# Loads that transpose, two channels in one matmul, and the plane sums moved into a 128-row contraction: one change of three parts to an attention and S4 kernel

## The chip, the cores and the metric

The kernel runs on one core of one Trainium2 chip. The metric is the device time of one execution in microseconds (us), median of several runs. Fast executions of a kernel agreed within about 1.5% here. The "granted clock" is the share of TensorE's full clock that the profile shows as allowed; in the traces here it is 1.00 or 0.5 at any moment, and a mean over a stretch lies between. "PE" is TensorE, "DVE" is VectorE, "ACT" is ScalarE, "POOL" is GpSimd and "SP" is SyncE, whose queue issues most of the loads.

## The reference, cut to what matters

The output joins two independent halves of 640 columns each.

```python
# half A: local dilated attention (32 heads of 20, window 8, dilation 2), S = 2048
qkv = x @ wqkv                                   # x [2048, 640]: needs x transposed for TensorE
o   = softmax(q . k_window * scale) . v_window;  a = o @ wo
# half B: S4 convolution, 640 channels d, 192 states n
K[d, l] = Re( sum_n C[d,n] * exp(dt*A)[d,n]**l * dt*B[d,n] )     # 2048 taps per channel
y = irfft( rfft(u, 4096) * rfft(K, 4096) )[:2048] + u * Dskip
```

The exponent `l` is rounded to bf16 before it is used, so many of the 2048 taps coincide. The kernel computes only distinct ones: a tap is a sum over n of X[n, a] * Y[n, b], with a table X of 20 powers and a table Y of 33 powers per channel, both complex and in bf16. So every channel costs TensorE a few very small matmuls: weights X (20 columns), moving data Y (33 columns). A matmul that needs only some of the 128 columns of TensorE's array can be placed on a part of them, a "column tile" of 32 or 64 columns (`tile_position` in the code). PSUM is the memory that matmuls write; ACT copies results out of it ("evictions").

## The kernel before

It works on five chunks of 128 channels (32 channels on each of four partition groups). Per chunk, DVE makes the tables X and Y; PE makes the taps (`kgen`); PE does a Fourier transform in two steps (`f1`, `f2_prod`); DVE multiplies the spectra of u and K; PE inverts (`ia`). The attention is interleaved with the chunks. A preparation stage of about 140 us comes first: parameters are loaded and flipped by PE ("flips", tile `ps_tr`), x is loaded and transposed by PE (`ps_xt`), projections of x are made (`ps_p`), and "generators" compute the tables' base powers. The order of instructions on each engine is not the order of the text: a scheduler decides it from modelled times, and then every engine executes in that order.

```python
def kgen(tc, pools, X, Y, Kd):                   # X [128, 20, 2, 192], Y [128, 33, 2, 192]
    for nt in (11, 11, 10):
        ps = psum.tile([128, nt, NB], f32, name="ps_k")
        MM(ps[:], lhsT=zw, rhs=Y[:, 0:nt, 0, 0:NB], start=True, stop=False)        # clears the bank
        for part in range(4):                    # real and imaginary; rows 0..127, then the last 64
            for i in range(nt):
                for g in range(4):
                    o = ps[32 * g:32 * g + 20, i, :]
                    if part < 2:
                        col = 32 * g + t0 + i
                        MM(o, lhsT=X[:, :, part, col], rhs=Y[:, :, part, col], ..., tile_position=(0, 32 * g))
                    else:
                        ...                      # 64 rows, tile_position=(hb, 32 * g)
        nc.scalar.copy(out=Kd[:, :, t0:t0 + nt], in_=ps[:]...)
    ...
# f2_prod: after S (both spectra, bf16) has been copied from PSUM by ACT
    V.tensor_tensor(out=Y, in0=K, in1=Ur..., op=A.mult)
    V.tensor_tensor(out=t[:], in0=K, in1=Ui..., op=A.mult)
    V.tensor_tensor(out=Y[:, :, 0], in0=Y[:, :, 0], in1=t[:, :, 1], op=A.subtract)
    V.tensor_tensor(out=Y[:, :, 1], in0=Y[:, :, 1], in1=t[:, :, 0], op=A.add)
# ia: weights of 32 columns, one column tile per group
            for r in range(2):
                for g in range(4):
                    MM(o, lhsT=Yf[:, :, r, 4 * j + g], rhs=C["EA"][:, r, :], ..., tile_position=(0, 32 * g))
# load and transpose
        for q in range(8):
            xn = xw.tile([128, 2, D], bf16, name="xn", bufs=3)
            nc.sync.dma_start(out=xn[:], in_=xsrc[:, 2 * q:2 * q + 2, :])
        ...                                      # later: 80 PE matmuls by the identity, 24 ACT copies into xT
```

The softmax here doesn't subtract the row's maximum and nothing guards it: scores larger than these inputs give would overflow.

Of the kernel before, what the change touches and what calls it, by code (L numbers as in the profile page):

```python
# [18 lines left out]
CW = 192  # L19
MAGIC = 12582912.0  # L20
# [8 lines left out]
X_EXP = [0, 4, 2, 6, 1, 5, 3, 7, 256, 260, 258, 262, 512, 516, 768, 772, 1024, 1280, 1536, 1792]  # L29
NB = 33  # L30
# [7 lines left out]
def sel_consts_np():  # L38
# [9 lines left out]
    def add(W):  # L48
        full = np.zeros((128, 128), np.float32)
        for g in range(4):  # L50
            full[32 * g:32 * g + 32, 32 * g:32 * g + 32] = W
        mats.append(full)
        return len(mats) - 1

    for j in range(8):
        Ws = {}
        for s in range(8):
            for be in range(32):
                p = 256 * s + 8 * be + j
                bhi, blo = be // 8, be % 8  # L60
                hit = [(i, b) for (i, b) in look[int(r[p])] if b == be or (b == be + 1 and i >= 8)]
                i, b = sorted(hit, key=lambda q: q[1])[0]
                W = Ws.setdefault((bhi, be % 2), np.zeros((8, 32, 32), np.float32))
                W[blo, i + 12 * (b - be), 4 * s + bhi] = 1.0
# [16 lines left out]
def fft_consts_np():  # L81
# [11 lines left out]
    EA = np.zeros((128, 2, 64, 2, 2))  # L93
    for dd in range(2):
        s = slice(64 * dd, 64 * dd + 64)
        EA[s, 0, :, 0, dd] = np.cos(phi)
        EA[s, 0, :, 1, dd] = np.sin(phi)
        EA[s, 1, :, 0, dd] = -np.sin(phi)
        EA[s, 1, :, 1, dd] = np.cos(phi)
    psi = 2 * np.pi * (l1[None, None, :] * k1[:, None, None] / 64 + l0[None, :, None] * k1[:, None, None] / 4096)  # L100
    HB = np.zeros((128, 64, 2, 128))
    for g in range(4):
        s = slice(32 * g, 32 * g + 32)
        HB[s, :, 0, s] = 2 * np.cos(psi) / 4096
        HB[s, :, 1, s] = -2 * np.sin(psi) / 4096
    return dict(BD1=BD1.reshape(128, 256), T=T.reshape(128, 32 * 2 * 64), EA=EA.reshape(128, 512), HB=HB.reshape(128, 64 * 2 * 128))


def partB_prep(tc, pools, prm, Gd):
# [29 lines left out]
    def flip(a, diag, tag="l"):  # L139
        psb = [psp.tile([128, 512], f32, name="ps_tr", tag=tag, bufs=2 if tag == "l" else 3) for _ in range(2)]  # L140
        for c in range(NCH):
            rhs = dg[:, c, :] if diag else ident[:]
            for h in range(2):
                hs = slice(64 * h, 64 * h + 64)
                col = c * CW + 64 * h
                nc.tensor.matmul(psb[col // 512][:, col % 512:col % 512 + 64], lhsT=nat[a][:, c, 0:128], rhs=rhs[:, hs], start=True, stop=True, skip_group_check=True)
            for h in range(2):
                hs = slice(64 * h, 64 * h + 64)
                col = c * CW + 128
                nc.tensor.matmul(psb[col // 512][hs, col % 512:col % 512 + 64], lhsT=nat[a][hs, c, 128:192], rhs=rhs[hs, hs], start=True, stop=True,  # L150
                                 tile_position=(64 * h, 64 * h), skip_group_check=True)
        return [(slice(0, 512), psb[0][:]), (slice(512, W), psb[1][:, 0:W - 512])]
# [62 lines left out]

def cmul(nc, O, Y, g, t, conj, rep=None):

    V = nc.vector
    sh = list(Y.shape)
    gr, gi = (g[:, r] for r in range(2))  # L220
    for _ in range(2):
        gr, gi = gr.unsqueeze(1), gi.unsqueeze(1)
    full = lambda ap: ap.rearrange("p a n r m -> p a (n r) m") if rep else ap
    gb = lambda ap: ap.to_broadcast([sh[0], sh[1], sh[2] * 2 if rep else 2, sh[-1]])
    V.tensor_tensor(out=full(O), in0=full(Y), in1=gb(gr), op=A.mult)  # L225
    V.tensor_tensor(out=full(t), in0=full(Y), in1=gb(gi), op=A.mult)  # L226
    P = [O[:, :, r] if not rep else O[:, :, :, r] for r in range(2)]
    T = [t[:, :, r] if not rep else t[:, :, :, r] for r in range(2)]
    V.tensor_tensor(out=P[0], in0=P[0], in1=T[1], op=(A.add if conj else A.subtract))  # L229
    V.tensor_tensor(out=P[1], in0=P[1], in1=T[0], op=(A.subtract if conj else A.add))  # L230


def table_tiles(pools):
    tp = pools["tab"]
    return (tp.tile([128, 20, 2, CW], bf16, name="Xtab", tag="Xtab", bufs=2), tp.tile([128, 6, 2, CW], bf16, name="Xg", tag="Xg"),
# [3 lines left out]
def tables(tc, pools, tiles):  # L239
# [3 lines left out]
    tmp = pools["tab"].tile([128, 8, 2, CW], bf16, name="krtmp", tag="krtmp")  # L243
# [3 lines left out]
    def xs(o, i, g):  # L247
        n = len(range(20)[i])
        cmul(nc, X[:, o], X[:, i], Xg[:, g], tmp[:, 0:n], True)

    S_ = slice
    xs(S_(1, 2), S_(0, 1), 2)
    xs(S_(2, 4), S_(0, 2), 1)
    xs(S_(4, 8), S_(0, 4), 0)
    xs(S_(8, 12), S_(0, 4), 3)
    cmul(nc, X[:, 12:16].rearrange("p (a b) r m -> p a b r m", a=2), X[:, 0:16].rearrange("p (a b) r m -> p a b r m", a=2)[:, :, 0:2], Xg[:, 4],
         tmp[:, 0:4].rearrange("p (a b) r m -> p a b r m", a=2), True, rep=2)
    xs(S_(16, 18), S_(0, 9, 8), 5)
    xs(S_(18, 20), S_(12, 15, 2), 5)
    for k in range(1, 5):  # L260
        n = 2 ** k - 1
        for i in range(0, n, 8):
            m = min(8, n - i)
            cmul(nc, Y[:, n + 2 + i:n + 2 + i + m], Y[:, 1 + i:1 + i + m], Y[:, n + 1], tmp[:, 0:m], False)
# [3 lines left out]
def kgen(tc, pools, X, Y, Kd):  # L268
    nc = tc.nc
    MM = nc.tensor.matmul  # L270
    t0 = 0
    for nt in (11, 11, 10):
        ps = pools["psum"].tile([128, nt, NB], f32, name="ps_k", tag="k", bufs=1)
        MM(ps[:], lhsT=pools["zw"], rhs=Y[:, 0:nt, 0, 0:NB], start=True, stop=False, skip_group_check=True)
        for part in range(4):
            for i in range(nt):
                for g in range(4):
                    o = ps[32 * g:32 * g + 20, i, :]
                    if part < 2:
                        col = 32 * g + t0 + i  # L280
                        MM(o, lhsT=X[:, :, part, col], rhs=Y[:, :, part, col], start=False, stop=False,  # L281
                           tile_position=(0, 32 * g), skip_group_check=True)
                    else:
                        col = 128 + 32 * (g % 2) + t0 + i
                        hb = 64 * (g // 2)
                        MM(o, lhsT=X[hb:hb + 64, :, part - 2, col], rhs=Y[hb:hb + 64, :, part - 2, col], start=False, stop=(part == 3),  # L286
                           tile_position=(hb, 32 * g), skip_group_check=True)
        nc.scalar.copy(out=Kd[:, :, t0:t0 + nt], in_=ps[:].rearrange("p t b -> p b t"))  # L288
        t0 += nt
    for g in range(4):  # L290
        r = 32 * g
        nc.gpsimd.dma_start(out=Kd[r + 20:r + 32, 0:NB - 1, :].rearrange("p b t -> p (b t)"), in_=Kd[r + 8:r + 20, 1:NB, :].rearrange("p b t -> p (b t)"))  # L292
# [35 lines left out]
def f2_prod(tc, pools, C, A1, Yf):  # L328
# [5 lines left out]
    for b in range(4):  # L334
        S = fp.tile([128, 8, 2, 2, 64], bf16, name="S", tag="S", bufs=2)
        for h in range(4):
# [7 lines left out]
            nc.scalar.copy(out=S[:, 2 * h:2 * h + 2], in_=ps[:])  # L344
        Y = Yf[:, 8 * b:8 * b + 8]
        K, Ur, Ui = S[:, :, :, 1, :], S[:, :, 0, 0, :], S[:, :, 1, 0, :]
        t = fp.tile([128, 8, 2, 64], bf16, name="pt", tag="pt", bufs=2)
        V.tensor_tensor(out=Y, in0=K, in1=Ur.unsqueeze(2).to_broadcast([128, 8, 2, 64]), op=A.mult)
        V.tensor_tensor(out=t[:], in0=K, in1=Ui.unsqueeze(2).to_broadcast([128, 8, 2, 64]), op=A.mult)
        V.tensor_tensor(out=Y[:, :, 0], in0=Y[:, :, 0], in1=t[:, :, 1], op=A.subtract)  # L350
        V.tensor_tensor(out=Y[:, :, 1], in0=Y[:, :, 1], in1=t[:, :, 0], op=A.add)


def ia(tc, pools, C, Yf, Z):
    nc = tc.nc
    MM = nc.tensor.matmul
    for jq in range(8):
        ps = pools["psum"].tile([128, 2, 64, 2, 2], f32, name="ps_ia", tag="b", bufs=3)
        for jj in range(2):
            j = 2 * jq + jj  # L360
            for r in range(2):
                for g in range(4):
                    o = ps[32 * g:32 * g + 32, jj].rearrange("p l r d -> p (l r d)")
                    MM(o, lhsT=Yf[:, :, r, 4 * j + g], rhs=C["EA"][:, r, :], start=(jj == 0 and r == 0), stop=(r == 1), skip_group_check=True, tile_position=(0, 32 * g))  # L364
# [13 lines left out]
class PartA:  # L378
# [8 lines left out]
    def load(self):  # L387
        nc, xw = self.nc, self.pools["xw"]
        xsrc = self.x[0].rearrange("(st p) k -> p st k", p=128)
        self.xn = []  # L390
        for q in range(8):
            xn = xw.tile([128, 2, D], bf16, name="xn", tag="xn", bufs=3)
            nc.sync.dma_start(out=xn[:], in_=xsrc[:, 2 * q:2 * q + 2, :])
            self.xn.append(xn)
# [7 lines left out]

    def transpose(self):
        nc, xw = self.nc, self.pools["xw"]
        self.xT = xT = xw.tile([128, 5, S], bf16, name="xT")
        for q in range(8):
            for kp in range(3):
                kn = 2 if kp < 2 else 1
                ps = self.psp.tile([128, 2, 2, 128], f32, name="ps_xt", tag="a", bufs=2)
                for kk in range(kn):  # L410
# [334 lines left out]
```

## Time and profile before

| | before |
|---|---|
| time | 511.86 us, median of 3 runs (510.85 over the 4 fast ones taken with the change) |
| PE / DVE / ACT busy, share of the span | 72% / 70% / 53% |
| granted TensorE clock, mean | 0.876 |
| first multiply of a table / first product of spectra | 58 us / 200 us |
| last tap matmul / end | 381.5 us / 511 us |

The busy line of the profile's page comes first, then the first steps of ACT and SP. In a timeline the columns are start, length, engine, line, operation, output <- input, shapes and count; the bracket tells how long the engine was idle and who released it.

```profile
...
PE 368.9 (72%) x5943; PEld 243.2 (48%) x5943; DVE 360.2 (70%) x528; ACT 269.0 (53%) x517; POOL 104.8 (21%) x192
...
```

```profile
...
17.56 0.59 ACT L168 CAST cc<-ps_tr 128x512 bf16<-128x512 f32 x1 [5.05 <-PE ps_tr L146]
18.04 1.08 ACT L414 CAST xT<-ps_xt 128x512 bf16<-128x512 f32 x2
...
33.14 0.59 ACT L414 CAST xT<-ps_xt 128x512 bf16<-128x512 f32 x1 [2.52 <-PE ps_xt L412]
33.62 0.46 ACT L208 ACTIVATE mc<-wi,quarter 128x192 int32<-128x192 int32 x1
...
```

```profile
...
5.18 2.17 SPq L393 DMA_DIRECT2D xn<-in_A_x_dram  x3
...
19.64 10.97 SPq L393 DMA_DIRECT2D xn<-in_A_x_dram  x5
...
```

ACT's copies of transposed x (`xT`) stand ahead of its first angle step (`mc`, at 33.6 us), with which the generators start; the loads of x come in two bursts, since only three buffers exist. Then the middle stage, by stretches. The columns are: stretch, its length, busy us with instruction counts of PE, its weight loads, DVE, ACT and POOL, granted clock, share of DMA, GB/s.

```profile
...
0.00:20.00 20.00, 8.01 (x76) 5.65 (x76) 6.04 (x15) 7.63 (x20) 14.62 (x41) 1.00 0.88 236
20.00:40.00 20.00, 14.97 (x127) 10.63 (x125) 5.09 (x9) 12.65 (x26) 4.47 (x6) 1.00 0.65 153
140.00:382.00 242.00, 186.90 (x3918) 134.52 (x3916) 221.72 (x302) 120.10 (x228) 26.19 (x57) 0.87 0.38 102
...
```

DVE is busy 221.7 of the 242 us from 140 to the last taps; it is what is waited for there. PE has 187 us of work in the same stretch: it is second, with some 55 us to spare. Last, the taps of one group of channels in PE's timeline:

```profile
...
182.20 1.65 PE L281 MATMUL ps_k<-Ytab,Xtab 128*20 128x33 bf16 x88
...
187.83 1.65 PE L281 MATMUL ps_k<-Ytab,Xtab 128*20 128x33 bf16 x88
...
194.37 1.69 PE L281 MATMUL ps_k<-Ytab,Xtab 128*20 128x33 bf16 x80
195.98 1.50 PE L286 MATMUL ps_k<-Ytab,Xtab 64*20 64x33 bf16 x80
...
```

Matmuls overlap, so the spacing of two starts is read as (length of the group - length of its last matmul) / (count - 1). A matmul here takes about 0.245 us from start to end, so (1.65 - 0.245) / 87 = 16 ns from one start to the next.

### The profile page before, as it was taken

The page shows a single profiled execution, that of the slowest core. Times are in us where ns is not written, and L with a number is a line of the kernel's source. Part 1 is how long each engine was busy: PE and PEld are TensorE (multiplying, and loading weights), DVE is VectorE, ACT ScalarE, POOL GpSimd, SP SyncE. Part 2 cuts the span into 40 slices and gives each one's busy share as a digit, 9 for nine tenths or more (in the row PEclk, how much of TensorE's full clock was granted, in tenths as well). Part 3 has the DMA queues.
Part 4 walks back from the last instruction along what each step waited for, and adds up shares of the span by engine and source line. Part 5 has one row for each costly group of instructions (what it writes and reads, how often), then busy time and mean ns, then how long its engine had stood idle before and what let it go on. Part 6 is the DMA issues. An engine that isn't in the chain of part 4 may idle for free.

```text
span 511.0 us, 13799 instructions
## 1 busy us (share of the span) xinstructions
PE 368.9 (72%) x5943; PEld 243.2 (48%) x5943; DVE 360.2 (70%) x528; ACT 269.0 (53%) x517; POOL 104.8 (21%) x192
## 2 busy tenths in 40 slices
PE   2868799874752778798879868699495855987720
PEld 1543334631220566666656755476263533765520
DVE  0326899651899997999999977998948753636012
ACT  4466895758682435656355723467224522656610
POOL 7605500055000001000170001070001341143012
PEclk9999999997795788799988978999779969997955
DMA  7964946359669352220236432043609597622262
GB/s 197 267 145 129 225 123 208 104 168 255 215 211 314 118 110 66 60 115 3 61 66 204 114 66 57 1 132 83 139 13 347 146 299 192 197 48 39 91 187 41
DMA packets 83596, 70.99 MB, mean 139 GB/s; under 512 B 51744, under 2 KB 75104, under 8 KB 81872
## 3 DMA queue, kind: packets, MB, share of 16 engines
q1 hardware_dynamic: 75456, 55.90, 39.0%
q0 software_dynamic: 6368, 13.16, 10.7%
q10 hardware_dynamic: 1712, 1.07, 0.8%
q8 instruction: 46, 0.75, 0.7%
q14 instruction: 14, 0.11, 0.1%
HBM read 42.86 MB, written 24.13 MB: 131 GB/s over the span
## 4 chain that ended last, share of the span: by engine, by line
PE 36%; DVE 28%; DMA 15%; ACT 12%; issue 6%; SPq 1%; POOL 0%; ACTq 0%; POOLq 0%; DVEq 0%
PE ps_o L493 6%; DVE krtmp L226 4%; PE ps_k L286 4%; PE ps_k L281 4%; PE ps_op L508 3%; DMA Gdram<-cs 3%; DMA xn<-in_A_x_dram 3%; PE ps_s L310 3%; ACT S L344 3%; DMA zq<-Zdram_61 3%; DMA out_dram<-ud 3%; DVE Ytab L225 3%; DVE prod L468 2%; PE ps_p L428 2%; DMA uq<-Udram 2%
## 5 line engine op out<-in xcount | busy, mean ns | idle before, releaser
L468 DVE TENSOR_TENSOR prod<-qb,kb 128x2048 bf16<-128x2048 bf16 x40 | 48.7, 1233 | 2.0 <-PE ps_l L471 2.0
L502 POOL DMA_DIRECT2D oT<-vb x64 | 36.7, 581 | 48.1 <-ACT vb L494 43.8
L429 ACT CAST st<-ps_p 128x512 bf16<-128x512 f32 x60 | 34.1, 581 | 12.6 <-PE ps_p L428 12.3
L428 PE MATMUL ps_p<-xT,w_324 128*128 128x512 bf16 x100 | 28.0, 439 | 13.7 <-ACT st L429 13.6
L364 PE MATMUL ps_ia<-cEA,Yf 128*32 128x256 bf16 x640 | 29.1, 333 | 7.9 <-DVE Yf L350 6.7
L494 ACT CAST vb<-ps_o 128x512 bf16<-128x512 f32 x20 | 13.1, 653 | 37.2 <-PE ps_o L493 37.1
L286 PE MATMUL ps_k<-Ytab,Xtab 64*20 64x33 bf16 x1280 | 25.8, 243 | 9.3 <-issue 9.2
L342 PEld LDWEIGHTS <-cT 128*64 128x64 bf16 x640 | 23.3, 114 | 18.9 <-issue 18.3
L288 ACT CAST Kd<-ps_k 128x363 bf16<-128x363 f32 (+1 forms) x15 | 6.8, 453 | 47.2 <-PE ps_k L286 47.2
L471 PE MATMUL ps_l<-prod,cGs 128*32 128x512 bf16 x160 | 18.3, 435 | 17.6 <-DVE prod L468 17.4
L225 DVE TENSOR_TENSOR Ytab<-Ytab 128x2688 bf16<-128x2688 bf16 (+3 forms) x25 | 30.8, 1234 | 0.0
L364 PEld LDWEIGHTS <-Yf 128*32 128x32 bf16 x640 | 23.3, 174 | 15.3 <-DVE Yf L350 8.2
L226 DVE TENSOR_TENSOR krtmp<-Ytab 128x2688 bf16<-128x2688 bf16 (+3 forms) x25 | 30.4, 1215 | 0.0
L281 PEld LDWEIGHTS <-Xtab 128*20 128x20 bf16 x1280 | 21.9, 125 | 14.9 <-issue 14.2
L493 PEld LDWEIGHTS <-cident 128*128 128x128 bf16 x160 | 14.9, 100 | 28.8 <-issue 14.4
L428 PE MATMUL ps_p<-xT,w_320 128*128 128x512 bf16 x100 | 25.6, 410 | 3.9 <-ACT st L429 2.8
L212 DVE TENSOR_TENSOR cs<-cs,am 128x768 bf16<-128x768 bf16 x22 | 12.2, 556 | 22.3 <-ACT cs L211 22.3
L292 POOL DMA_DIRECT2D Kd<-Kd x20 | 10.1, 514 | 86.6 <-ACT Kd L288 86.2
L286 PEld LDWEIGHTS <-Xtab 64*20 64x20 bf16 x1280 | 21.9, 121 | 12.2 <-issue 10.6
L244 POOL MEMSET Ytab<- 128x192 bf16 x5 | 1.4, 284 | 123.9 <-PE ps_k L286 123.9
L225 DVE TENSOR_TENSOR Xtab<-Xtab,Xg 128x768 bf16<-128x768 bf16 (+2 forms) x35 | 24.7, 706 | 2.2 <-DMA Xg<-Gdram 1.8
L281 PE MATMUL ps_k<-Ytab,Xtab 128*20 128x33 bf16 x1280 | 25.1, 246 | 1.1 <-DVE Ytab L229 0.5
(460 smaller groups left out, 948.7 us busy)
## 6 DMA issues: line engine op xcount, KB each, us to landing
HB<-k_HB SPq DMA_DIRECT2D x8, 1024.0 KB, 6.1
Gdram<-cs SPq DMA_DIRECT2D x24, 192.0 KB, 3.1
kb<-kd SPq DMA_DIRECT2D x4, 710.0 KB, 6.7
vb<-vd SPq DMA_DIRECT2D x4, 710.0 KB, 5.4
xn<-in_A_x_dram SPq DMA_DIRECT2D x8, 320.0 KB, 6.0
us<-in_B_u_dram POOLq DMA_DIRECT2D x16, 160.0 KB, 5.0
Udram<-uc POOLq DMA_DIRECT2D x8, 320.0 KB, 4.0
kd<-st SPq DMA_DIRECT2D x5, 512.0 KB, 5.8
```

What stands on the lines that cost most here:

```text
L225: V.tensor_tensor(out=full(O), in0=full(Y), in1=gb(gr), op=A.mult)
L226: V.tensor_tensor(out=full(t), in0=full(Y), in1=gb(gi), op=A.mult)
L281: MM(o, lhsT=X[:, :, part, col], rhs=Y[:, :, part, col], start=False, stop=False, tile_position=(0, 32 * g), skip_group_check=True)
L286: MM(o, lhsT=X[hb:hb + 64, :, part - 2, col], rhs=Y[hb:hb + 64, :, part - 2, col], start=False, stop=(part == 3), tile_position=(hb, 32 * ...
L342: nc.tensor.matmul(ps[64 * dd:64 * dd + 64, kk, r], lhsT=T[:, k, r, :], rhs=A1[:, k, :, 64 * dd:64 * dd + 64], start=(kk == 0 and r == 0), ...
L364: MM(o, lhsT=Yf[:, :, r, 4 * j + g], rhs=C["EA"][:, r, :], start=(jj == 0 and r == 0), stop=(r == 1), skip_group_check=True, tile_position ...
L428: nc.tensor.matmul(ps[:], lhsT=w[:, kt, 128 * ct:128 * ct + 128], rhs=self.xT[:, kt, 512 * sc:512 * sc + 512], start=(kt == 0), stop=(kt = ...
L429: nc.scalar.copy(out=st[:, sc], in_=ps[:])
L468: V.tensor_tensor(out=pr[:], in0=q[:, ct].unsqueeze(1).to_broadcast([128, 4, 4, 128]), in1=windows(k[:, ct, :, 8 - 8 * m:8 - 8 * m + 128], ...
L471: nc.tensor.matmul(ps[32 * sc:32 * sc + 32], lhsT=self.pools["Gs"][:, ct, :], rhs=pr[:, :, sc, :], start=(ct == 0), stop=(ct == 4), tile_p ...
L493: nc.tensor.matmul(ps[:], lhsT=self.ident[:], rhs=p2[:, w], start=(w == 0), stop=(w == W - 1))
L502: nc.gpsimd.dma_start(out=oT[32 * q:32 * q + 32, :, sc, :], in_=self.vb[qb][32 * sc:32 * sc + 32, q:DH:4, HALO:HALO + 128])
```

## The change

Three parts, each meant to take work away.

1. **x by DMA.** Eight transposing loads of 320 KB each write x transposed directly. 80 PE matmuls, 24 ACT copies and the buffers go.
2. **Two channels per tap matmul.** X and Y of two channels (index e) are read together: 40 weight columns, 66 moving columns, and of the four 20 x 33 blocks the two on the diagonal are used. 256 matmuls per chunk instead of 512, on two column tiles of 64 instead of four of 32. The constants and the layouts of the tables follow.
3. **Plane products.** The sums of the complex product leave DVE: all four products (Ur*Kr, Ur*Ki, Ui*Kr, Ui*Ki) are stored, and the inverse adds them in PSUM, with a constant EA of four planes instead of two. The inverse now uses 128 weight columns on the whole array: 64 matmuls per chunk instead of 128.

The core of the diff, with cuts:

```diff
@@ kgen
-    for nt in (11, 11, 10):
-        ps = pools["psum"].tile([128, nt, NB], f32, name="ps_k", tag="k", bufs=1)
-        MM(ps[:], lhsT=pools["zw"], rhs=Y[:, 0:nt, 0, 0:NB], start=True, stop=False, skip_group_check=True)
+    Xr = X[:].rearrange("p r a (e m) -> p r (a e) m", e=2)
+    Yr = Y[:].rearrange("p b r (e m) -> p e b r m", e=2)
+    for nt in (7, 7, 6, 6, 6):
+        ps = pools["psk"][:, 0:nt * 2 * NB].rearrange("p (t e b) -> p t e b", e=2, b=NB)
         for part in range(4):
             for i in range(nt):
-                for g in range(4):
-                    ...
+                for h in range(2):
+                    o = ps[64 * h:64 * h + XROWS, i]
+                    rows = slice(0, 128) if part < 2 else slice(64 * h, 64 * h + 64)
+                    col = t0 + i + (32 * h if part < 2 else 64)
+                    MM(o, lhsT=Xr[rows, part % 2, :, col], rhs=Yr[rows, :, :, part % 2, col], ...,
+                       tile_position=(0 if part < 2 else 64 * h, 64 * h), skip_group_check=True)
@@ f2_prod
-        V.tensor_tensor(out=Y[:, :, 0], in0=Y[:, :, 0], in1=t[:, :, 1], op=A.subtract)
-        V.tensor_tensor(out=Y[:, :, 1], in0=Y[:, :, 1], in1=t[:, :, 0], op=A.add)
+        for i, u in enumerate((Ur, Ui)):
+            V.tensor_tensor(out=Yf[:, 2 * i:2 * i + 2, :, 32 * b:32 * b + 32], in0=K, in1=u..., op=A.mult)
@@ ia
-            for r in range(2):
-                for g in range(4):
-                    MM(o, lhsT=Yf[:, :, r, 4 * j + g], rhs=C["EA"][:, r, :], ..., tile_position=(0, 32 * g))
+            for q in range(4):
+                nc.tensor.matmul(ps[:, jj]..., lhsT=Yf[:, q, 2 * jq + jj, :], rhs=C["EA"][:, q, :], ...)
@@ load
-            nc.sync.dma_start(out=xn[:], in_=xsrc[:, 2 * q:2 * q + 2, :])
+            nc.sync.dma_start(out=self.xT[:, :, 256 * q:256 * q + 256], in_=self.x[0, 256 * q:256 * q + 256, :], transpose=True)
... (the transposing matmuls and copies, the flips' column order, table layouts and constants are cut)
```

## The prediction

> **What bounds the kernel now.** The stage table (20 us stretches) shows three parts. (1) 0-140 us, preparation: VectorE (DVE) is busy 6.0 and 5.1 us in the first two; PE and ScalarE (ACT), in order, wait behind loading and PE-transposing x (loads issued until 30.6 us, because three buffers recycle), so ACT's first angle copy starts at 33.6 us and the first table at 58. Later ACT paces the generators. (2) 140-382 us: DVE busy about 222 of 242 us. (3) 382-511 us: PE, chained loads and output; DVE under half busy.
>
> **What changes, costed from the trace.**
> - Plane products: 20 subtractions and 20 adds of 128x512 leave DVE (8.4 + 8.8 = 17.2 us, 3.4 per chunk). The 40 multiplies of 0.69 us stay.
> - Table X: eight complex multiplies instead of seven, same elements: four more fixed costs of about 0.15 us per chunk (0.35 us at 384 elements, 0.56 at 768), +2.8 us; PSUM clear +0.6. Net DVE -14 us.
> - Inverse: 128 matmuls of 32 weight columns on four column tiles become 64 on the full array. Before: 6.3 us per chunk cold (208.9-215.2), about 36 ns each warm. The spread matmuls have the new shape and run at 100 ns: 6.5 us per chunk warm, 9 starting cold. PE +2 to +3 us per chunk.
> - Tap matmuls: 512 pairs per chunk become 256, with 40 weight columns and 66 moving. Pairs now run 18 ns apart (88 in 1.58 us). I read no fixed issue cost there: the first Fourier matmuls, 64 strided weight columns, run 57 ns apart; the second, 64 contiguous ones and the same moving size, 28. Strided weights thus cost about 0.9 ns per column, and 256 x 35 = 9 us replaces 512 x 18 = 9.2. This agrees with the Trainium skill (TensorE: Matmul & The Clock Gate, LDWEIGHTS: time follows columns, not rows). Won: the clearing matmuls (1 us per chunk) and some issue gaps (1-2 us); five evictions through one bank instead of three give 2 us back.
> - x: 80 PE matmuls, 24 ACT copies (12 us) and the buffer waits go; eight transposing loads of 320 KB come. The Trainium skill (DMA: Bandwidth & Descriptors, Latency and other measured facts) gives 261 GB/s with a split middle dimension: an estimate of 10 us alone; amid 88% DMA load 20-25, landing near 28 us. No run yet shows it. The new order puts seven projection evictions, needing all of x, ahead of that angle copy, so it starts about when it does now, that work already done.
>
> **On the critical path.** Part 1: -5 us. Part 2: 3 x 3.4, less 2.2, plus 3 us of shorter waits: -11. Part 3: products -1 to -3, inverse +2 to +3, taps -2: about -2. Sum about -19 us.
>
> **Predicted: 492 us, range 473 to 513. Faster by over 2%: 0.70, within 2%: 0.21, slower: 0.09.**
>
> **What would show it.** The Yf multiplies stay at 0.69 us, the 0.42 us groups vanish; DVE busy 346 us. Tap matmuls near 35 ns apart (18 would refute the weight-load reading). Inverse matmuls 100-107 ns apart, ACT copies unchanged at 0.6 us. x landed by 30 us; first table by 55.
>
> **What would make it wrong.** Transposing loads much slower than plain ones: ACT and PE wait in order, part 1 grows 10-30 us. A cold clock in the inverse (213 ns each). Issue-limited tap matmuls (towards 480). Tap evictions stuck in ACT's queue.

## More of the kernel before

Unless a place says otherwise, all times are of undisturbed ("fast") runs.

Note how the taps' operands lie: a channel is one index of the last axis of 192, so the 20 weight columns and the 33 moving columns of one matmul are each one element out of every 384. They are read with a stride.

A chunk's 512 tap matmuls cost 8.2 us.

## The result, and the profile after

The changed kernel took **558.03 us** (median of 4 fast runs, 557.57 to 559.22), against 510.85 for the kernel before on the same chip: **slower by 9.3%** (ratio 1.0928, 95% interval 1.0891 to 1.0964). Every ratio in this document is the mean time of one kernel's fast runs over that of the kernel before's fast runs of the same rounds, so not quite the ratio of the medians quoted. Executions over 1.5% slower than the fastest of the same kernel are left out of the means.

| | before | after |
|---|---|---|
| time (us) | 510.85 | 558.03 |
| PE / DVE / ACT busy (us) | 369 / 360 / 269 | 416 / 343 / 264 |
| first multiply of a table (us) | 58 | 67.5 |
| first product of spectra (us) | 200 | 227 |
| last tap matmul (us) | 381.5 | 430.4 |
| granted clock, mean | 0.876 | 0.793 |

The same views of the kernel after, in the same order. The busy line:

```profile
...
PE 415.8 (75%) x4272; PEld 277.6 (50%) x4272; DVE 343.3 (62%) x509; ACT 264.3 (48%) x503; POOL 104.5 (19%) x191
...
```

DVE lost 17 us of work, as meant. PE gained 47 us, with 1671 instructions fewer: by tiles, the taps with their clearing matmuls rose from 55.0 to 86.8 us and the inverse (`ps_ia`) from 29.1 to 40.5, the 11.1 us of x transposes went, and `ps_o`, attention matmuls that the change does not touch, rose from 41.6 to 52.0 (more on these under "Not settled"). The first steps of ACT and SP, and what PE waited for in the first 70 us (in the view of waits: engine, tile and line that waited <- whom for: us in total, times, longest):

```profile
...
29.45 0.56 ACT L182 CAST cc<-ps_tr 128x480 bf16<-128x480 f32 x1 [16.98 <-PE ps_tr L164]
29.91 0.59 ACT L419 CAST st<-ps_p 128x512 bf16<-128x512 f32 x1
...
43.93 0.58 ACT L419 CAST st<-ps_p 128x512 bf16<-128x512 f32 x1 [0.49 <-PE ps_p L418]
44.41 0.46 ACT L222 ACTIVATE mc<-wi,quarter 128x192 int32<-128x192 int32 x1
...
```

```profile
...
5.14 26.53 SPq L397 DMA_TRANSPOSE xT<-in_A_x_dram  x8
...
```

```profile
...
DVE pr L188 <- PE ps_tr L164: 25.5, 2, 25.3
...
ACT cc L182 <- PE ps_tr L164: 19.5, 4, 17.0
...
PE ps_p L418 <- DMA xT<-in_A_x_dram: 14.1, 2, 9.5
...
```

The eight transposing loads occupy SP's queue from 5.1 to 31.7 us. The last of them lands at 35.7 us (issued at 30.1, landing 5.6 later); the last plain load landed at 34.2 (30.2 and 4.0), so x as a whole came hardly later. PE has projections of x in its order ahead of most of the flips, and waits 14.1 us in two waits for x. The flips, which do not need x, stand behind that; so ACT's first copy of a flip (`cc`) comes at 29.5 us after an idle 17, and DVE waits 25.5 us for flips. The first angle step comes at 44.4 us; it came at 33.6. The stretches:

```profile
...
0.00:20.00 20.00, 4.70 (x48) 3.11 (x48) 5.90 (x16) 5.39 (x15) 12.97 (x37) 1.00 1.00 152
20.00:40.00 20.00, 14.53 (x82) 6.87 (x82) 0.00 (x0) 4.48 (x8) 4.60 (x9) 1.00 0.94 230
160.00:431.00 271.00, 223.58 (x2674) 163.62 (x2675) 212.43 (x291) 122.55 (x231) 26.02 (x57) 0.75 0.30 83
...
```

From 20 to 40 us DVE does nothing at all. In the first stretch the DMA engines are fully taken (1.00) but move 152 GB/s, where they moved 236 at 0.88. In the middle stretch, which is now 271 us long, PE has 224 us of work and DVE 212: neither is busy all the time. The taps in PE's timeline:

```profile
...
197.39 1.10 PE L295 MATMUL ps_k<-Ytab,Xtab 128*40 128x66 bf16 x14
...
202.34 3.71 PE L295 MATMUL ps_k<-Ytab,Xtab 128*40 128x66 bf16 x56
...
211.46 3.16 PE L295 MATMUL ps_k<-Ytab,Xtab 128*40 128x66 bf16 x48
...
414.09 3.69 PE L295 MATMUL ps_k<-Ytab,Xtab 128*40 128x66 bf16 x56
...
```

A matmul of these takes about 0.30 us from start to end. (1.10 - 0.30) / 13 = 62 ns from start to start, (3.71 - 0.30) / 55 = 62 ns, (3.16 - 0.30) / 47 = 61 ns. (The two longer groups hold matmuls of 128 rows and then of 64; by single starts the first kind is at about 61 ns and the second at 57.) A chunk's 256 cost 15.7 us and not 8.2. The clock is not the reason: 56 such matmuls took 3.69 us where the granted clock stood at 0.50 (414 to 418 us), and 3.71 us where it stood at 0.98 (202 to 206 us). The starts of single matmuls in the trace tell more: in most groups of the kernel after they come in pairs within about 4 ns, and then nothing for some 110 to 130 ns; in the kernel before they come by fours, and then nothing for about 57 ns. A pair, or a four, has one matmul on each column tile.

### The profile page after: what moved, and what is told of

It reads as the page before. It is cut to its first block, busy times and chain, and to the rows that moved or that the text cites. A ratio compares the mean times of both kernels' runs of the same rounds, so it can differ in the third digit from the quotient of the medians.

```text
span 556.0 us, 10440 instructions
## 1 busy us (share of the span) xinstructions
PE 415.8 (75%) x4272; PEld 277.6 (50%) x4272; DVE 343.3 (62%) x509; ACT 264.3 (48%) x503; POOL 104.5 (19%) x191
## 4 chain that ended last, share of the span: by engine, by line
PE 31%; DVE 9%; ACT 5%; DMA 5%; issue 2%; SPq 0%; POOL 0%; POOLq 0%; DVEq 0%; ACTq 0%
PE ps_k L295 9%; PE ps_o L483 8%; PE ps_ia L369 3%; ACT S L356 3%; PE ps_op L498 3%; DMA out_dram<-ud 2%; PE ps_s L322 2%; DMA zq<-Zdram_61 1%; DVE krtmp L234 1%; PE ps_l L461 1%; DMA vb<-vd 1%; DVE Ytab L234 1%; PE ps_ib L657 1%; ACT A_5837 L337 1%; DVE ud L662 1%
## 5 line engine op out<-in xcount | busy, mean ns | idle before, releaser
L295 PEld LDWEIGHTS <-Xtab 128*40 128x40 bf16 (+1 forms) x1280 | 75.2, 152 | 29.8 <-issue 28.1
L295 PE MATMUL ps_k<-Ytab,Xtab 128*40 128x66 bf16 (+1 forms) x1280 | 86.8, 300 | 1.5 <-DVE Ytab L235 0.7
L461 PE MATMUL ps_l<-prod,cGs 128*32 128x512 bf16 x160 | 20.5, 429 | 57.5 <-DVE prod L458 57.4
L297 ACT CAST Kd<-ps_k 128x396 bf16<-128x396 f32 (+1 forms) x25 | 13.1, 524 | 78.9 <-PE ps_k L295 78.9
L369 PE MATMUL ps_ia<-cEA,Yf 128*128 128x256 bf16 x320 | 40.5, 288 | 1.8 <-DVE Yf L359 1.8
L418 PE MATMUL ps_p<-xT,w_337 128*128 128x512 bf16 x100 | 27.7, 427 | 16.1 <-DMA xT<-in_A_x_dram 14.1
L359 DVE TENSOR_TENSOR Yf<-S 128x1024 bf16<-128x1024 bf16 x40 | 26.0, 685 | 22.3 <-ACT S L356 22.1
L369 PEld LDWEIGHTS <-Yf 128*128 128x128 bf16 x320 | 32.7, 103 | 10.4 <-DVE Yf L359 3.2
L461 PEld LDWEIGHTS <-cGs 128*32 128x32 bf16 x160 | 4.9, 94 | 63.3 <-issue 61.0
L484 ACT CAST vb<-ps_o 128x512 bf16<-128x512 f32 x20 | 11.7, 585 | 39.4 <-PE ps_o L483 30.3
L418 PE MATMUL ps_p<-xT,w_341 128*128 128x512 bf16 x100 | 28.0, 438 | 0.0
L222 ACT ACTIVATE mc<-wi,quarter 128x384 int32<-128x384 int32 (+1 forms) x33 | 18.4, 558 | 18.5 <-DVE ph L223 18.4
```

Source lines behind the costliest of these rows:

```text
L222: nc.scalar.activation(out=mc, in_=wi[:, s], func=ACT.Identity, bias=pools["quarter"][:, k:k + 1])
L295: MM(o, lhsT=Xr[rows, part % 2, :, col], rhs=Yr[rows, :, :, part % 2, col], start=(part == 0 and i == 0), stop=(part == 3), tile_position= ...
L359: V.tensor_tensor(out=Yf[:, 2 * i:2 * i + 2, :, 32 * b:32 * b + 32], in0=K, in1=u.unsqueeze(1).to_broadcast([128, 2, 16, 32]), op=A.mult)
L369: nc.tensor.matmul(ps[:, jj].rearrange("p l r d -> p (l r d)"), lhsT=Yf[:, q, 2 * jq + jj, :], rhs=C["EA"][:, q, :], start=(jj == 0 and q ...
L418: nc.tensor.matmul(ps[:], lhsT=w[:, kt, 128 * ct:128 * ct + 128], rhs=self.xT[:, kt, 512 * sc:512 * sc + 512], start=(kt == 0), stop=(kt = ...
L461: nc.tensor.matmul(ps[32 * sc:32 * sc + 32], lhsT=self.pools["Gs"][:, ct, :], rhs=pr[:, :, sc, :], start=(ct == 0), stop=(ct == 4), tile_p ...
```

## The experiments

The theory: the taps' matmuls became four times as far apart and only half as many; x by DMA delays the preparation, because of what queues behind it in order; the plane products do what they should. The rivals are named at each run. There were twelve different kernels, and all passed the comparison with the reference. That comparison is too coarse to vouch for the taps: three kernels with taps that are wrong on purpose passed too.

### One part alone, and in pairs

`only_x`, `only_products` and `only_taps` are the kernel before with one part of the change (its hunks of the diff); `x_products` is the kernel before with the parts 1 and 3, that is, the change without its taps:

```diff
 only_x:         -  nc.sync.dma_start(out=xn[:], ...); PE transposes      +  dma_start(..., transpose=True)
 only_products:  -  subtract and add in f2_prod, two-plane EA             +  four-plane Yf, EA and HB; 64 matmuls in ia
 only_taps:      -  20x33 taps on four column tiles                       +  40x66 taps on two, tables and constants to match
 x_products:     -/+ as only_x and only_products together
```

> Kernel before with x loaded by the transposing loads and nothing else of the change. Main theory (the tap matmuls are the loss): about +5 to +10 us over before, 515 to 521 us, because the first table starts later (after: 67.5 us against 58.2) and little of it cascades. Rival (the late x is the main loss and cascades through the preparation): +20 us or more, 531 or above. The first projection matmul should again wait until about 21 us, and the first table start near 67 us.

> Kernel before with only the four plane products, the sum inside the inverse's contraction and its constants. Main theory: faster by 8 to 15 us, 496 to 503 us, since DVE loses 17 us of adds, about 10 of them in the stretch where DVE is the limit, and PE gains 2 to 3 us per chunk. Rival (the full-array inverse delays PE, which is what made the changed kernel slow): 511 us or slower.

> Kernel before with only the two-channel tap matmuls and the table layout that they need. Main theory: this is nearly the whole loss, +35 to +55 us, 546 to 566 us, with tap matmuls 66 ns apart as in the changed kernel (18 ns before). Rival (late x): +0 to +15 us.

> The changed kernel with the old tap matmuls and tables: transposing loads and plane products together. Main theory: the two effects add, so about -10 to +2 us, 501 to 513 us. Rival (late x): 525 us or above.

Later, `taps_x` ran the change without its plane products. (The third pair, taps and products with x loaded as before, did not fit in the on-chip memory and was never run.)

> The whole change without its plane products. Single effects so far: transposing loads +10.7 us, taps +41.7, products -11.7; their sum is 6 to 7 us below the whole change's +47. If the missing microseconds lie between taps and loads (both delay the first table and the first spectra), this run comes at 567 to 574 us, and the products are worth their 11.7 us inside the change too. The rival: the products are worth less there, because TensorE and not VectorE is waited for in the chunks, then this run is at 560 to 565 us (no interaction of taps and loads, products worth 3 to 6 us).

Measured, the ratio to the kernel before of the same rounds:

| parts in it | median (range), us | ratio, 95% interval |
|---|---|---|
| x | 520.78 (516.75-522.48) | 1.0202 (1.0120-1.0284) |
| products | 498.39 (496.63-499.63) | 0.9763 (0.9681-0.9845) |
| taps | 551.73 (550.65-555.43) | 1.0834 (1.0753-1.0915) |
| x, products | 511.71 (510.02-512.77) | 1.0033 (0.9962-1.0103) |
| x, taps | 567.12 (563.98-568.64) | 1.1109 (1.1046-1.1171) |
| x, products, taps (the change) | 558.03 (557.57-559.22) | 1.0928 (1.0891-1.0964) |

With 1% of the kernel before worth 5.1 us: the products gain 12 us alone, 9 us with x, and 9 us with x and taps; x costs 10 us alone and 14 us with the products or with the taps; the taps cost 43 us alone, 46 us with x, and 46 us with x and products. The intervals are 2 to 4 us wide to either side, so x alone is clearly slower and products alone clearly faster, but whether by more than 2% is unclear for both, and differences of 3 to 5 us between such figures are not clear of noise. So nothing hidden in the combination is needed to explain the 47 us: it is the taps, then x, less the products, with interactions of a few microseconds at most. (What x costs turns out below to be two things of opposite sign.) The rival that I set for `taps_x`, that the products are worth little once PE is the engine waited for, is not decided: 9 us, give or take 4, is between its 3 to 6 and the 11.7 that I held it against. All five times came out inside the range of the theory named first (`taps_x` at its edge); two details did not, since the first table of `only_x` came at 63 us and not near 67, and the taps of `only_taps` were 61 to 62 ns apart and not 66.

How the taps reach the end of the kernel is seen in what DVE waited for in the middle, from 140 us (160 in the whole change) to the last taps: first in the kernel before, then in `only_taps`, then in the whole change.

```profile
...
DVE Yf L348 <- ACT S L344: 8.0, 5, 3.7
DVE p_5051 L490 <- PE ps_o L493: 2.3, 1, 2.3
DVE rc L481 <- PE ps_n L479: 2.0, 2, 1.5
...
```

```profile
...
DVE rc L491 <- PE ps_n L489: 17.0, 2, 12.6
DVE p L500 <- PE ps_o L503: 16.6, 5, 8.9
DVE Yf L358 <- ACT S L354: 9.4, 5, 4.2
DVE prod L478 <- PE ps_l L481: 5.5, 3, 3.6
...
```

```profile
...
DVE prod L458 <- PE ps_l L461: 12.6, 2, 12.3
...
DVE p_3771 L480 <- PE ps_o L483: 8.0, 1, 8.0
DVE p_2762 L480 <- PE ps_o L483: 7.0, 1, 7.0
DVE p_4797 L480 <- PE ps_o L483: 6.2, 1, 6.2
...
```

All waits of DVE for PE in that stretch come to 4.9 us in the kernel before and to 39.1 us in `only_taps` (summed over the view; 41.8 us in the whole change). The attention's small matmuls (`ps_o`, `ps_n`, `ps_l`) stand behind the taps in PE's order, and DVE waits for them. PE is not simply full (it is idle for 47 of the 271 us of the change's middle stage): the added tap time counts where it comes before something that DVE waits for. That part of these waits is the lower clock of `ps_o` is not excluded (see "Not settled").

### Why the taps are 62 ns apart

What differs from 16 ns: two column tiles instead of four, 40 weight columns instead of 20, 66 moving columns instead of 33. Three kernels with wrong taps take these apart. Each ran once, so only spacings inside its trace are used.

`tiles_1_2_4`, on the kernel before: part 0 goes to one column tile, part 1 to two, parts 2 and 3 stay on four.

```diff
-                    if part < 2:
-                        MM(o, lhsT=X[:, :, part, col], rhs=Y[:, :, part, col], ..., tile_position=(0, 32 * g))
+                    if part == 0:
+                        MM(ps[0:20, i, :], ..., tile_position=(0, 0))
+                    elif part == 1:
+                        MM(ps[32 * (g % 2):32 * (g % 2) + 20, i, :], ..., tile_position=(0, 32 * (g % 2)))
```

> Wrong result on purpose. Kernel before, its 20x33 tap matmuls unchanged in size and strides, but the first 44 of each group go to one column tile, the next 44 alternate between two, the last 88 use four as before. Theory (each column tile does load and matmul one after the other, and the tiles run side by side, so the spacing is a tile's cycle divided by the number of tiles): 72 ns, 36 ns and 18 ns apart. Rival (the written reading: a weight load takes about 0.9 ns per strided column on one shared path): 18 ns in all three.

PE's timeline (L283 is one tile, L286 two, L289 four):

```profile
...
185.38 2.61 PE L283 MATMUL ps_k<-Ytab,Xtab 128*20 128x33 bf16 x42 [0.15 <-DVE Ytab L229]
...
187.88 1.59 PE L286 MATMUL ps_k<-Ytab,Xtab 128*20 128x33 bf16 x42
...
196.52 1.65 PE L289 MATMUL ps_k<-Ytab,Xtab 64*20 64x33 bf16 x88
...
```

(2.61 - 0.235) / 41 = 58 ns on one tile, (1.59 - 0.24) / 41 = 33 ns on two, (1.65 - 0.24) / 87 = 16 ns on four. Times the number of tiles that is 58, 66 and 65 ns: a tile needs some 58 to 66 ns for one 20 x 33 matmul with its weights, whatever the others do, and the tiles work side by side. My numbers for it were a little high (72, 36, 18); the rival, a fixed spacing of 18, is refuted. Halving the number of tiles is by itself a doubling of the spacing.

`contiguous`, on the kernel after: part 0 reads packed weights, part 1 packed moving data, part 2 both, part 3 neither (the values are then wrong, sizes and tiles are the same).

```diff
+                    Wc = X[rows, part % 2, t0 + i - (20 if t0 + i >= 20 else 0), 0:40]
+                    Mc = Y[rows, t0 + i, part % 2, 0:2 * NB].rearrange("p (e b) -> p e b", e=2)
+                    if part == 0:   MM(o, lhsT=Wc, rhs=M, **fl)
+                    elif part == 1: MM(o, lhsT=W, rhs=Mc, **fl)
+                    elif part == 2: MM(o, lhsT=Wc, rhs=Mc, **fl)
+                    else:           MM(o, lhsT=W, rhs=M, **fl)
```

> Wrong result on purpose. Changed kernel, tap matmuls of the same sizes on the same two tiles; part 0 reads its 40 weight columns contiguously, part 1 its 66 moving columns, part 2 both, part 3 neither. Theory (a tile's cycle of about 133 ns is a strided weight load of about 38 ns plus a strided moving read of about 95): weights contiguous 48 to 55 ns apart, moving contiguous about 38, both 20 to 30, neither 66. Rival (weight load alone): weights contiguous 30 or less, moving contiguous still 66.

```profile
...
105.99 0.97 PE L300 MATMUL ps_k<-Ytab,Xtab 128*40 128x66 bf16 x14
106.77 0.62 PE L302 MATMUL ps_k<-Ytab,Xtab 128*40 128x66 bf16 x14
107.32 0.39 PE L304 MATMUL ps_k<-Ytab,Xtab 64*40 64x66 bf16 x14
107.55 0.98 PE L306 MATMUL ps_k<-Ytab,Xtab 64*40 64x66 bf16 x14
...
```

The four lines are packed weights (L300), packed moving data (L302), both (L304) and neither (L306). With 14 matmuls each: (0.97 - 0.292) / 13 = 52 ns; (0.62 - 0.236) / 13 = 29.5 ns; (0.39 - 0.19) / 13 = 15.4 ns; (0.98 - 0.29) / 13 = 53 ns. The last two lines have 64 rows, the first two 128; 128 rows with neither packed are the first group of the kernel after above, 62 ns. So the stride of the moving data is worth about 32 ns of the 62, the stride of the weights about 9, and with both packed (on 64 rows) the spacing is a quarter. The 9 are less certain than the 32: the same shape with neither packed came to 53 ns on 64 rows here and to 62 on 128. The rival, that the weight load alone sets the spacing, is refuted: it is the smaller part. Packed moving data and both packed came out lower than I expected (38, and 20 to 30). And packing shows the clock: with both packed, two groups at a granted clock of 0.50 (from 378.0 and 382.9 us) had 25 ns from start to start and not 15, while the strided taps kept their spacing.

The Trainium skill has the reason in words (Advanced Engine Details and Errata, section SBUF Cachelines): on-chip memory is read by lines of 16 bytes, and a read pattern that touches a different line with every element pays for it. Here every element of both operands is on a line of its own: the moving elements of a channel are 768 bytes apart. The runs agree that strided operands are the slow ones, and put numbers on it that the page does not have; that the 16-byte line is the reason was not tested, since no run had a smaller stride.

`sizes`, on the kernel after: two tiles throughout, other sizes.

```diff
+                    if part == 0:   MM(o[0:20], lhsT=W[:, 0:20], rhs=M, **fl)             # 20 x 66
+                    elif part == 1: MM(o[:, 0], lhsT=W, rhs=M[:, 0], **fl)                # 40 x 33
+                    elif part == 2: MM(o[0:20, 0], lhsT=W[:, 0:20], rhs=M[:, 0], **fl)    # 20 x 33, 64 rows
+                    else:           MM(o, lhsT=W, rhs=M, **fl)                            # 40 x 66, 64 rows
```

> Wrong result on purpose. Changed kernel, same two tiles and strides; part 0 has 20 weight columns and 66 moving, part 1 40 and 33, part 2 20 and 33, part 3 40 and 66. Theory (cycle of a tile = load + matmul, divided by two tiles): about 57, 45, 36 and 66 ns apart. Rival (a fixed cost per matmul): 66 in all four.

```profile
...
252.12 0.98 PE L298 MATMUL ps_k<-Ytab,Xtab 128*20 128x66 bf16 x14
...
253.35 0.72 PE L300 MATMUL ps_k<-Ytab,Xtab 128*40 128x33 bf16 x14
254.00 0.59 PE L302 MATMUL ps_k<-Ytab,Xtab 64*20 64x33 bf16 x14
254.52 1.02 PE L304 MATMUL ps_k<-Ytab,Xtab 64*40 64x66 bf16 x14
...
```

The lines are 20 x 66 (L298), 40 x 33 (L300), 20 x 33 (L302) and 40 x 66 on 64 rows (L304). They give 53, about 37, 27 and 55 ns (each (length - last) / 13, with last matmuls of 0.29, 0.25, 0.23 and 0.29 us). The kernel after's 40 x 66 on 128 rows is at 62. Leaving out 33 moving columns takes 62 - 37 = 25 ns off on two tiles, 50 ns per tile, an estimate of 1.5 ns per strided moving column. Leaving out 20 weight columns takes 62 - 53 = 9 ns off, 18 ns per tile, an estimate of 0.9 ns per strided weight column. I had expected 57, 45, 36 and 66. The rival, a fixed cost per matmul, would have shown four equal spacings, and is refuted.

Together: one tile's turn is about the weight load plus the matmul, each by its strided columns (an estimate, each price from one difference of sizes). In the kernel before that is 20 x 0.9 + 33 x 1.5 = 67 ns, and the trace shows 65 on four tiles: 16 ns each. In the kernel after the same sum gives 40 x 0.9 + 66 x 1.5 = 135 ns, and the trace shows 123 on two tiles, 62 each; so the two prices hold to some 10%, or 15% against the 58 ns of one tile alone. The change made a turn twice as long, halved the number of turns that go side by side, and halved the number of matmuls: in sum twice the time. Half of what the larger matmuls compute, the products between different channels, is thrown away.

### What x by DMA costs, and why

`x_flips_first` starts from `x_products`. The key weights of the projections get a false dependency on the last result of the flips, so that the scheduler cannot put projections ahead of them; their load also moves from ACT's queue to SP's:

```diff
-            (nc.scalar if i == 1 else nc.gpsimd).dma_start(out=t[:], ...)
+            if i == 1:
+                nc.vector.tensor_copy(out=t[:, 0, 0:1], in_=Gt[:, 4, 1, 0:1])
+            (nc.sync if i == 1 else nc.gpsimd).dma_start(out=t[:], ...)
```

> Kernel x_products (transposing loads, plane products, old taps), with the load of the key weights made to wait for the kernel parameters' product, so that no projection can stand ahead of the parameter transposes on PE. Theory (the transposing loads cost time because PE and ACT, in order, wait for x ahead of the parameter work): first table by 50 us instead of about 67, total 493 to 503 us, 10 to 18 under x_products. Rival (the loads themselves are too slow or crowd out the other loads): 508 us or above.

It took 496.63 us (493.89 to 501.29, ratio 0.9789, 0.9702 to 0.9876): 15 us below `x_products`, with the same transposing loads. The flips were done at 21.6 us and the first table was begun at 53 us (63.5 in `x_products`; I had expected it by 50). (The repeat below gives 491.57 and ratio 0.9617, so the gain over `x_products`, by the ratios, is 12 to 21 us.) So the loss was not in the loads' own time but in what the order put behind them. What remained: the key weights were now issued at 35.1 us on SP's queue, behind the eight loads, and ACT stood with copies of projections in its order.

`flips_first_pool_queue` therefore loads the key weights from GpSimd's queue, which has none of the eight loads:

```diff
-            (nc.sync if i == 1 else nc.gpsimd).dma_start(out=t[:], ...)
+            nc.gpsimd.dma_start(out=t[:], ...)
```

It ran on one chip with repeats of `x_flips_first` and `only_products`, five rounds each, to see which version is the best.

> The transposing loads and the plane products, with before's taps; the key weights wait for the parameter flips as in x_flips_first, but are loaded by the GpSimd queue and not behind the eight transposing loads. If the late key weights (issued at 35.1 us there) were what held ScalarE's angle steps up, the first table multiply comes at 45 to 50 us (53.2 there) and the time is 2 to 6 us below x_flips_first: 490 to 495 us. Rival: x itself lands only at 38 to 42 us, the projections' copies still hold ScalarE, and the time stays within 2 us of x_flips_first.

> A repeat of x_flips_first beside only_products: 494 to 501 us. If the loads by transposing are worth anything once the flips go first (64 copies fewer on ScalarE and 128 multiplies fewer on TensorE), it is 1 to 3 us below only_products of the same call; if not, the two are equal within 1 us.

> A repeat of only_products beside the two versions with early flips, to decide the best: 496 to 500 us.

| kernel | fast runs: median (range), us | ratio, 95% interval |
|---|---|---|
| flips_first_pool_queue | 485.02 (482.24-487.44) | 0.9489 (0.9444-0.9535) |
| x_flips_first_again | 491.57 (489.19-493.30) | 0.9617 (0.9566-0.9667) |
| only_products_again | 499.24 (494.13-500.86) | 0.9747 (0.9694-0.9800) |

```profile
...
5.11 34.30 SPq L387 DMA_TRANSPOSE xT<-in_A_x_dram  x8
...
```

```profile
...
38.93 0.35 DVE L227 TENSOR_TENSOR Xtab<-Xtab,Xg 128x384 bf16<-128x384 bf16 x1
...
```

```profile
...
0.00:20.00 20.00, 10.77 (x104) 6.93 (x104) 6.79 (x17) 9.27 (x21) 15.35 (x42) 1.00 0.98 168
20.00:40.00 20.00, 6.91 (x34) 2.86 (x33) 14.16 (x45) 9.94 (x23) 3.54 (x5) 1.00 1.16 188
...
```

The repeat of `x_flips_first` came out better than expected, 7.7 us below the repeat of `only_products` where 1 to 3 were expected. (Its expectation miscounts: 24 copies and 80 matmuls go, not 64 and 128.) `flips_first_pool_queue` is the fastest of all versions, 25 us below the kernel before. DVE is busy 14.2 us between 20 and 40 us, where the changed kernel shows 0.00, and its first table multiply comes at 38.9 us. Both of my numbers were too cautious: I expected 45 to 50 us for that multiply, and 490 to 495 us in all. The transposing loads hold SP's queue even longer here, 34.3 us. The rival, that the late arrival of x still holds ACT's angle steps up, is refuted.

One question was left: does the transposing load gain anything here, or only the flips that go first, which a kernel with PE transposes could have too? And is the order what x costs inside the whole change? Three more runs on one chip. `products_flips_first` is `only_products` with an identity for the transposes of x that is copied after the flips' last result, and four buffers for x instead of three (more do not fit). `change_flips_first` is the whole change with the same edit as `flips_first_pool_queue`.

```diff
 products_flips_first:
+        nc.vector.tensor_copy(out=id2[:, 0:1], in_=self.Gt[:, 4, 1, 0:1])
+        nc.vector.tensor_copy(out=id2[:], in_=self.ident[:])
-                        nc.tensor.matmul(ps[:, kk, i, :], lhsT=self.xn[q]..., rhs=self.ident[:], ...)
+                        nc.tensor.matmul(ps[:, kk, i, :], lhsT=self.xn[q]..., rhs=id2[:], ...)
 change_flips_first:
+            if i == 1:
+                nc.vector.tensor_copy(out=t[:, 0, 0:1], in_=Gt[:, 4, 1, 0:1])
-            (nc.scalar if i == 1 else nc.gpsimd).dma_start(out=t[:], ...)
+            nc.gpsimd.dma_start(out=t[:], ...)
```

> only_products (PE transposes of x, before's taps) with the flips put first: the transposing matmuls need an identity that is copied only after the flips' last result, and x has four buffers instead of three. If the order is all that matters, this gains as much as the transposing loads with flips first: 483 to 488 us. If the loads by DMA are worth their 24 ACT copies (12 us) and 80 PE matmuls, some of that shows: 490 to 497 us. The copies of transposed x stand among ACT's angle steps here, and wait for x's later buffers.

> A repeat beside products_flips_first on the same chip: 482 to 488 us.

> The whole change, with nothing altered but that the key weights wait for the flips and are loaded from GpSimd's queue. If order is what makes x cost 14 us in the change, the first table multiply comes at 38 to 45 us (67.5 in the change) and the time falls by 15 to 27 us to 531 to 543 us. If the taps on PE hide the preparation, less than 8 us come back: above 550 us.

| kernel | fast runs: median (range), us | ratio, 95% interval |
|---|---|---|
| products_flips_first | 497.53 (495.73-500.56) | 0.9753 (0.9707-0.9799) |
| flips_first_pool_queue_again | 485.50 (482.03-489.19) | 0.9500 (0.9449-0.9552) |
| change_flips_first | 530.16 (526.91-530.51) | 1.0360 (1.0300-1.0419) |

`products_flips_first` is as fast as `only_products` and no faster, just outside both of my expectations. Its first table multiply came at 39.3 us, so the early start is there; but it was lost again. The waits from 80 to 140 us suggest where, first of `products_flips_first` and then of `flips_first_pool_queue_again`:

```profile
...
DVE cs L214 <- ACT cs L213: 25.0, 9, 12.0
...
```

```profile
...
DVE cs L214 <- ACT cs L213: 11.1, 9, 2.1
...
```

With PE transposes, ACT's copies of projections run from 52 to 155 us; with transposing loads, from 38 to 139. The generators of the later chunks (`cs`) share ACT with them, in order, and DVE waits 25.0 us for them against 11.1 (21.6 in `only_products`). That this wait is the whole loss was not tested. So each half needs the other: the order alone gains nothing here, the loads alone cost 14 us beside the products, and both together gain 12 us over `only_products` (485.50 against 497.53 for `products_flips_first`, which equals it).

`change_flips_first` gave back 28 us of the change's 47 (530.16 against 558.03; by the ratios, 5.7% or 29 us), just beyond the 15 to 27 that I expected; its first table multiply came at 41.1 us. The edit changes two things, the order and the queue of the key weights, and no run parts them inside the whole change. What remained above `flips_first_pool_queue_again`, 44.7 us, is the taps.

## Why the prediction was wrong, point by point

**Right: the plane products.** The prediction said that "the 40 multiplies of 0.69 us stay" and that DVE's busy time falls to 346 us. The trace after shows 40 multiplies of 0.685 us, no subtractions and adds, and 343.3 us. The inverse's matmuls came out at about 109 ns in most groups (40 in 4.53 us from 296.4 us on, the last of them 0.28), close to the predicted 100 to 107, and the first chunk's 64, which started at a low clock, took 9.8 us where 9 were predicted. This part alone gained 12 us, and 9 us inside the change; the prediction's terms for it (-10.2 in part 2, -1 to -3 and +2 to +3 in part 3) come to about -10.

**Wrong, and most of the miss: the taps.** The step that failed is "Strided weights thus cost about 0.9 ns per column, and 256 x 35 = 9 us replaces 512 x 18 = 9.2." The 0.9 ns per weight column agree with `sizes` in the figure alone: I read it as spacing (57 ns for 64 columns), and `sizes` shows it for one tile, 0.45 ns of spacing with two. Two things were left out. First, the moving data is strided too; the two Fourier matmuls from which I took the figure both stream packed data, so they could not show it, though the skill's section on cachelines would have warned. A strided moving column costs about 1.5 ns, more than a weight column (`contiguous`, `sizes`). Second, before ran its turns on four tiles side by side, and after on two; I compared spacings without multiplying by the number of tiles (`tiles_1_2_4`). The prediction measured 18 ns and I took it as the price of 20 weight columns at 0.9; that agreement was chance. The trace shows 62 ns where 35 were predicted, and 15.7 us per chunk instead of 9. Five chunks make 37 us more on PE (by the busy time of tile `ps_k`, 32 us with the saved clearing matmuls counted), and taps alone cost 43 us.

The prediction leaned on the Trainium skill there (TensorE: Matmul & The Clock Gate, section LDWEIGHTS): a weight load takes time by its columns and not by its rows. The runs agree in the main, 18 ns per tile for 20 columns fewer; rows were not varied alone. But the same page says in another section (Wait — 56ns, not 53.3ns?) that start-to-start "never drops below ≈25 ns however small N is". The trace of the kernel before had 16 ns, on four tiles, in plain view: that alone said that tiles run side by side, and that a number from two tiles may not be carried to four. The page TensorEngine Tiling (Array Packing), section Key Properties, states just this: "Tiles operate independently: Different tiles can execute LdWeights and Matmul in parallel". I did not use it. That factor of tiles is what the change gives away.

**Wrong: "PE" was not taken as the next bound.** The prediction put part 2 wholly on DVE ("DVE busy about 222 of 242 us"), and so it could not price a PE that grows. PE had 55 us to spare there, and the average hid that DVE waits for particular matmuls behind the taps: with about 8 us more per chunk, DVE's waits for PE grew from 4.9 to 41.8 us in that stretch.

**Wrong: x.** The step was "an estimate of 10 us alone; amid 88% DMA load 20-25, landing near 28 us" with the order of ACT's evictions "that work already done", part 1 at -5 us. x alone cost +10. The loads took SP's queue until 31.7 us and the last landed at 35.7, so the size was too small by some 8 us. The larger error is in what stands behind it: the prediction followed ACT's order only. In PE's order the projections stand before the parameter flips, so the wait for x became a wait of the flips, of ACT (17 us) and of DVE (25 us), and the first angle step came 11 us later and not "about when it does now". My list of what would make it wrong named this ("ACT and PE wait in order, part 1 grows 10-30 us"), but the range gave it too little weight. `change_flips_first` shows that this order (with the queue of the key weights), and not the DMA's bandwidth, is what costs: the same loads, with the flips first, brought the change from 558 to 530 us. The intent itself was sound. Without the taps and with the flips first the kernel runs in 485 us, below the 492 predicted.

**Not settled.** The mean clock fell from 0.876 to 0.793. PE's long idle stretch before the first inverse (44 us in one wait for DVE, from 135 to 178 us) goes along with a low clock (0.5 from 137.6 to 195.6 us). The taps kept their spacing, but other matmuls did not: those of `ps_o` start 216 ns apart where the granted clock is 1.00 and 426 where it is 0.5. In the change 58 of the 160 started at 0.5, and in the kernel before 12; in the four kernels with the new taps as they stand 29 to 58 did, and in every kernel with the old taps 8 to 18. In `contiguous`, the changed kernel with the operands of its taps partly packed, 14 did, and its single run took 519.74 us (state unknown, so an indication and no verdict). So a lower clock comes with the slow taps, and the 43 to 46 us that they cost contain what it costs, some 10 us of PE time in `ps_o`. No run took the clock alone away, so its share of the end time is open. Nor was a correct version with packed table operands tried: DVE would have to write both tables with another stride, and that cost is unmeasured. Interactions of 3 to 5 us between the parts were not followed further.

## What to carry to other kernels

Before you merge small matmuls, work out a tile's turn (weight load plus stream, by columns, strided ones at their measured price) and divide by the number of column tiles that work side by side: fewer matmuls on half the tiles can take twice the time. A spacing read from one kind of matmul may be used only for the same number of tiles and the same strides of both operands. When a load gets slower or moves, look at every in-order engine for work that stands behind it without needing it; a false dependency that puts that work first, with the queue that goes with it, gave back 28 us here.

## What the Trainium skill lacked or had wrong

- TensorE: Matmul & The Clock Gate, section Wait — 56ns, not 53.3ns?: start-to-start is said never to fall below about 25 ns. With matmuls of 20 x 33 on four column tiles the runs show 16 ns, and 15.4 ns for 40 x 66 with both operands packed, 64 rows on two tiles, at a granted clock of 1.00. The floor may hold per tile (58 ns on one tile, and two times 15.4 ns, do not contradict it); it does not hold across tiles, and the section does not say so.
- Advanced Engine Details and Errata, section SBUF Cachelines, says that touching a new 16-byte line with every element has a penalty, without a size, and TensorE: Matmul & The Clock Gate, section Back-to-back issue gap, gives the spacing of matmuls without it. The runs show about 32 ns of a 62 ns spacing for strided moving data on two tiles (an estimate of 1.5 ns per strided column and tile) and about 9 ns for strided weights.
- TensorEngine Tiling (Array Packing), section Key Properties, is right that tiles load weights and multiply in parallel, but has no measured number for it. The runs show 58, 33 and 16 ns for a matmul of 20 x 33 on one, two and four column tiles.
- Advanced Engine Details and Errata, section X-Bar Transpose (TRN2), says that transposing DMAs "are as fast as regular DMAs". Eight of them, 2.6 MB in all, held SP's queue for 26.5 us beside other loads, and the DMA engines moved 152 GB/s at a share of 1.00 in the first 20 us, where the plain loads gave 236 GB/s at 0.88. No run measured them alone, so this neither shows nor refutes the sentence.
